# Scores 2 and 3 right behind the sums in four of six blocks, and a batch's fourth block with the last gate ahead of a convolution

## Chip, cores and metric

The kernel runs on one core of a Trainium2 chip. The metric is the device time of one execution in microseconds; the median of the runs counts. One execution was also recorded by the hardware profiler, and all rows below are of that one.

## What is computed

Capped softmax attention over 8 batches, 12 heads, 448 positions and 64 elements a head, and behind it a gated feed-forward layer with a causal convolution of five steps. `cap` is 30, so the largest score can be replaced by the cap in the exponential's shift.

```python
# attention
scores = cap * tanh(q @ k.T / sqrt(64) / cap)
attn = exp(scores - max(scores))
x = attn / (sum(attn) + 1e-9) @ v                # heads side by side: (8, 448, 768)
# layer
gate_pre[s] = sum over k of conv_w[k] * x[s - 4 + k]      # five steps, per column
gate = 1 / (1 + exp(-gate_pre))
out = (gate * (x @ w_val)) @ w_out
```

## The kernel before

The 48 pairs of heads are 48 blocks, six to a batch. For each block the kernel does these steps, each a function of its own in `fast_path`:

- `load`, `turn`: q and k come from memory (SyncE issues the DMAs) and are transposed on VectorE. `half_hi` (ScalarE) rounds them to the type that TensorE takes in one pass, `half_lo` (VectorE) makes the difference.
- `scores(p, i)`, i from 0 to 3: TensorE, keys on 112 rows, both heads at once on 64 rows of the array each; from block 13 on six matmuls each (high by high, high by low, low by high). They go to one of two PSUM tiles `pss`, so that scores 2 and 3 need what tanh 0 and 1 have read.
- `tanh`, `exp`: ScalarE, from `pss` to `pt`, then in place. There are six `pt` buffers.
- `add(p, 0)` adds the exponentials of i = 0 and 1, `add(p, 1)` those of 2 and 3, `add(p, 2)` these two: VectorE, in the tiles `pa0` and `pa1`.
- `attnv(p, i)`: TensorE, attention by v into `psa`; `sums`: a matmul with ones on the last `add` into `psz`, one for each head.
- `turn_sums`, `norm_recip`, `spread`, `norm_mul`: VectorE, the reciprocal of the sums, spread over the rows, times `psa`; the product `u` is x transposed. `x_hi` (ScalarE) and `x_lo` (VectorE) split x in two parts, `conv` (VectorE) makes the five steps of the convolution from `u`.

For a batch there is the layer: `sigmoid` of six gates (ScalarE), `val` (TensorE, six groups of 36 matmuls in two parts of 18), `gate` (VectorE, the product of the two), `gated_hi` (ScalarE) and `gated_lo` (VectorE), the two parts of the product, `out_part` (TensorE, six groups in even batches, eight in odd ones, each in two parts of 18), `store` (ScalarE copies from PSUM) and `store_out` (SyncE). `val` and `out_part` share two PSUM tiles `psf`. GpSimd has `keep_tail` alone, a copy once in two batches.

The order on each engine is written out by hand: every step gets a time in units of blocks from a table (`STEADY`, `SPLIT` and others; 0.62 in block p's table means p + 0.62), all are sorted by it, and each engine runs its own steps in that order and waits where data or a buffer is missing. So a block's steps lie between p - 1.9 (its load) and p + 1.9 (the end of its convolution), and the steps of three neighbours stand between one another. In block p's own stretch, from `scores(p, 0)` at p to the next block's, stand `attnv` and `sums` of block p - 1 (at p + 0.10 to p + 0.28), and with p + 0.36 and p + 0.74 two groups of 18 matmuls each of `val` or `out_part`; scores 2 and 3 stand between these two, at p + 0.62. `val` of a batch lies in the stretches of the next batch's first four blocks, `out_part` in those of its fourth to sixth and of the first after these. Behind block 47 there are no scores, and `val` and `out_part` of the last batch run by themselves.

For blocks from 12 on that are the first of their batch, `LATE_X` puts x's difference and the convolution late in the next block's stretch, where the sigmoids and two gates stand.

Of the kernel before, what the change touches and what calls it, by code (L numbers as in the profile page):

```python
# [82 lines left out]

SIXTH = PAIRED | {k: EARLY[k] for k in ("tq", "tk", "scores", "tanh", "exp")} | {"add": (0.38, 0.62)}

LATE_X = {"x_lo": 1.76, "conv": (1.78, 1.80, 1.83, 1.86, 1.89)}
NEARLY, NPAIRED, NPLAIN = 6, 11, 13

# [99 lines left out]
def fast_path(tc, io, u2, q, k, v, w_val, conv_w, w_out, out, capt):  # L188
# [8 lines left out]
    NPAIR = H // 2  # L197
    NP = B * NPAIR
# [12 lines left out]
    with ExitStack() as ctx:  # L211
# [82 lines left out]
        def half_hi(name, p):  # L294
            st = state[p]
            st[name, "h"] = scratch["qk"].tile([P, S], F32R, name=name + "h")
            nc.scalar.copy(st[name, "h"], st[name])

        def half_lo(name, p):
            st = state[p]  # L300
            st[name, "l"] = scratch["qk"].tile([P, S], F32R, name=name + "l")
            less(nc.vector, st[name, "l"], st.pop(name), st[name, "h"])
# [175 lines left out]
        tables = [EARLY if p < NEARLY else SIXTH if p == NEARLY else PAIRED if p < NPAIRED else STEADY if p < NPLAIN else SPLIT for p in range(NP)]  # L478
        for p in range(NPAIRED, NP):
            if p % NPAIR == 0:  # L480
                tables[p] = tables[p] | LATE_X

        def at(when, f, *a):
            events.append((when, len(events), f, a))

# [5 lines left out]
            q_hi=lambda p: half_hi("q", p), k_hi=lambda p: half_hi("k", p),  # L491
            q_lo=lambda p: half_lo("q", p), k_lo=lambda p: half_lo("k", p),
            scores=scores, tanh=tanh, exp=exp, add=add, av=attnv, sums=sums, turn_sums=turn_sums, recip=norm_recip,
            spread=spread, mul=norm_mul, x_hi=x_hi, x_lo=x_lo, conv=conv,
        )
        for p, table in enumerate(tables):
            for name, f in steps.items():
                x = table.get(name, ())
                if isinstance(x, tuple):
                    for i, y in enumerate(x):  # L500
                        at(p + y, f, p, i)
                else:
                    at(p + x, f, p)
        for b in range(B):
            t0 = NPAIR * b
            for d in range(NCC):
                sig = SIG_AT if b else SIG_FIRST
                y = (VAL if b else VAL_FIRST)[d]
                at(t0 + sig, sigmoid, b, d)
                for i in range(PARTS):  # L510
                    at(t0 + y + i * PART, val, b, d, i)
                done = t0 + max(y + PARTS * PART, sig + 0.17)
                at(done + 0.01, gate, b, d)

                last = d == NCC - 1
                at(done + (0.02 if last else 0.08), gated_hi, b, d)
                at(done + (0.03 if last else 0.12), gated_lo, b, d)
            if b % 2 == 0:
                at(t0 + KEEP_AT, keep_tail)
            for m, y in enumerate(OUT_ODD if b % 2 else OUT_LATE if b == B - 2 else OUT_EVEN):  # L520
                for i in range(PARTS):
                    at(t0 + y + i * PART / 2, out_part, b, m, i)
                at(t0 + y + 0.20, store, b, m)
                at(t0 + y + 0.40, store_out, b, m)
# [139 lines left out]
def kernel(tc, q, k, v, cap, w_val, conv_w, w_out, out):  # L664
    nc = tc.nc
    with tc.tile_pool(name="cap_pool", bufs=1) as pool, tc.tile_pool(name="io", bufs=2) as io:
        capt = pool.tile([P, 1], F32, name="capt")
        nc.sync.dma_start(capt, cap.rearrange("(o c) -> o c", o=1).partition_broadcast(P))

        pad = conv_w.shape[0] - 1  # L670
        u2 = [pool.tile([P, pad + q.shape[2]], F32, name=f"u{i}") for i in range(2)]
        for t, src in zip(u2, (q, k)):
            load_blocks(nc, t[:, pad:], src, 0)
        mag = pool.tile([1, 1], F32, name="mag")
        nc.vector.scalar_tensor_tensor(mag, capt[0:1], -1.0, capt[0:1], ALU.mult, ALU.max)
        small = pool.tile([1, 1], I32, name="small")
        nc.vector.tensor_scalar(small, mag, CAP_FAST, None, ALU.is_le)
        flag = nc.values_load(small, min_val=0, max_val=1)
        with tc.If(flag != 0) as cmp:
            fast_path(tc, io, u2, q, k, v, w_val, conv_w, w_out, out, capt)  # L680
        with cmp.Else():
            general_path(tc, q, k, v, w_val, conv_w, w_out, out, capt)
# [30 lines left out]
```

## Time and profile before

| | |
|---|---|
| median of 3 runs | 750.18 us (749.81 to 752.12) |
| the profiled execution | 749.64 us, span 747.9 us |
| TensorE busy, matmuls | 724.3 us |
| VectorE busy | 593.0 us |
| ScalarE busy | 537.7 us |
| mean granted clock of TensorE | 0.997 |

The span runs from the first to the last instruction of the profile; what lies around it belongs to the execution's time as well. Up to about 175 us the weights are prepared beside the first twelve blocks; from there to 688 us every stretch of a block is between 13 and 17 us long; behind 688 us comes the last batch's layer. An engine's busy time is the time covered by its instructions. A matmul counts from its start to its modelled end, and the next one starts before that end, so the distance between starts tells the rate. "Idle before" is time between an instruction and the one ahead of it, with the instruction that ended it.

### The profile page before, as it was taken

How to read it: one execution, taken by the hardware profiler on the slowest of the kernel's cores; microseconds unless marked ns; L12 is line 12 of the kernel's file. 1: busy time of each engine (PE TensorE's matmuls, PEld its weight loads, DVE VectorE, ACT ScalarE, POOL GpSimd, SP SyncE). 2: the span in 40 equal slices, each digit the busy share in tenths (PEclk: the TensorE clock that was granted, in tenths of full speed). 3: DMA queues.
4: the chain of work that ended last, by engine and by line, in shares of the span. 5: the costliest groups of instructions: out<-in, count | busy, mean ns of one | idle time of the engine just before them, and what ended most of it. 6: DMA issues, size and time to landing. Idle time of an engine off the chain costs nothing.

```text
span 747.9 us, 10860 instructions
## 1 busy us (share of the span) xinstructions
PE 724.3 (97%) x3972; PEld 488.3 (65%) x3972; DVE 593.0 (79%) x972; ACT 537.7 (72%) x708; POOL 9.0 (1%) x16
## 2 busy tenths in 40 slices
PE   5899998999999999999999999999999999999997
PEld 2333655566667776676777766667667775775997
DVE  2799899888987789987998679988898778997320
ACT  5899967778776697677857677687976659674311
POOL 0000001000000000000000000000000000000000
PEclk9999999999999999999999999999999999999999
DMA  6998867853223232233322333233322332210001
GB/s 105 234 212 195 209 166 149 232 110 73 37 51 79 70 73 37 61 82 71 67 46 61 88 69 54 38 81 73 59 49 62 80 79 41 49 35 22 22 21 67
DMA packets 241820, 63.75 MB, mean 85 GB/s; under 512 B 228448, under 2 KB 235616, under 8 KB 241760
## 3 DMA queue, kind: packets, MB, share of 16 engines
q1 hardware_dynamic: 241760, 62.98, 38.1%
q8 instruction: 33, 0.54, 0.3%
q14 instruction: 27, 0.22, 0.1%
HBM read 51.94 MB, written 11.01 MB: 84 GB/s over the span
## 4 chain that ended last, share of the span: by engine, by line
PE 43%; DVE 25%; ACT 16%; issue 4%; SPq 1%; DMA 1%; DVEq 0%; ACTq 0%
PE psf L461 8%; PE pss L312 7%; PE psf L463 7%; PE psf L462 7%; PE psa L349 6%; DVE pa L334 5%; ACT pt L320 5%; ACT pt L324 4%; DVE gate L411 4%; PE psz L361 3%; ACT gate L417 2%; PE psf L432 2%; DVE g_l L226 2%; PE psf L433 2%; PE psf L434 2%
## 5 line engine op out<-in xcount | busy, mean ns | idle before, releaser
L320 ACT ACTIVATE pt<-pss,rc 112x896 f32<-112x896 f32 x192 | 185.6, 1003 | 28.7 <-PE pss L312 28.7
L324 ACT ACTIVATE pt<-pt,capt 112x896 f32<-112x896 f32 x192 | 189.2, 1038 | 0.1
L349 PE MATMUL psa<-pt,vn 112*64 112x448 f32 x720 | 146.9, 546 | 0.0
L411 DVE SCALAR_TENSOR_TENSOR gate<-u,cw,gate 128x448 f32<-128x448 f32 x192 | 132.4, 690 | 5.8
L461 PE MATMUL psf<-wo,g_h 128*128 128x384 f32 x336 | 117.6, 350 | 0.0
L463 PE MATMUL psf<-wo,g_l 128*128 128x384 f32 x336 | 113.3, 337 | 0.0
L462 PE MATMUL psf<-wo,g_h 128*128 128x384 f32 x336 | 113.2, 337 | 0.0
L432 PE MATMUL psf<-xh,wv 128*128 128x448 f32 x288 | 108.8, 378 | 0.1
L434 PE MATMUL psf<-xl,wv 128*128 128x448 f32 x288 | 104.4, 362 | 0.0
L433 PE MATMUL psf<-xh,wv 128*128 128x448 f32 x288 | 104.3, 362 | 0.0
L334 DVE TENSOR_TENSOR pa<-pt 112x896 f32<-112x896 f32 x84 | 91.1, 1084 | 13.3 <-ACT pt L324 13.3
L349 PEld LDWEIGHTS psa<-pt,vn 112*64 112x64 f32 x720 | 47.4, 136 | 81.2 <-issue 69.8
L395 ACT CAST xh<-u 128x448 fp32r<-128x448 f32 x48 | 27.1, 565 | 77.1 <-DVE u L390 77.0
L461 PEld LDWEIGHTS psf<-wo,g_h 128*128 128x128 f32 x336 | 63.4, 189 | 22.0 <-issue 17.7
L369 DVE STREAM_TRANSPOSE zt<-psz 128x448 f32<-128x448 f32 x45 | 28.9, 641 | 56.3 <-PE psz L361 56.3
L432 PEld LDWEIGHTS psf<-xh,wv 128*128 128x128 f32 x288 | 54.0, 187 | 25.9 <-issue 18.3
L463 PEld LDWEIGHTS psf<-wo,g_l 128*128 128x128 f32 x336 | 63.6, 189 | 0.3
L462 PEld LDWEIGHTS psf<-wo,g_h 128*128 128x128 f32 x336 | 63.6, 189 | 0.0
L312 PE MATMUL pss<-qt,kt 64*112 64x448 f32 x208 | 49.6, 593 | 13.4 <-DVE guard L235 7.9
L441 ACT CAST g_h<-gate 128x448 fp32r<-128x448 f32 x48 | 26.3, 562 | 47.4 <-DVE gate L438 47.3
L469 ACT COPY osb<-psf 128x384 f32<-128x384 f32 x56 | 26.7, 478 | 45.9 <-PE psf L463 43.2
L312 PE MATMUL pss<-qh,kh 64*112 64x448 f32 x280 | 58.5, 412 | 0.0
(74 smaller groups left out, 904.2 us busy)
## 6 DMA issues: line engine op xcount, KB each, us to landing
vn<-in_v_dram SPq DMA_DIRECT2D x96, 112.0 KB, 2.6
out_dram<-osb SPq DMA_DIRECT2D x56, 192.0 KB, 1.9
qn<-in_q_dram SPq DMA_DIRECT2D x188, 56.0 KB, 2.5
kn<-in_k_dram SPq DMA_DIRECT2D x188, 56.0 KB, 2.4
w_raw<-in_moe_w_val_dram SPq DMA_DIRECT2D x12, 384.0 KB, 4.5
w_late<-in_moe_w_val_dram SPq DMA_DIRECT2D x12, 384.0 KB, 4.3
w_raw<-in_moe_w_out_dram SPq DMA_DIRECT2D x12, 384.0 KB, 3.7
w_late<-in_moe_w_out_dram SPq DMA_DIRECT2D x12, 384.0 KB, 4.7
```

The lines of the kernel that those rows point to most:

```text
L312: nc.tensor.matmul(ps[:CH, j, :S], st[x][r, c], st[y][r], start=(n == 0), stop=(n == len(parts) - 1))
L320: nc.scalar.activation(st["p", i], st.pop(("s", i)), AF.Tanh, scale=rc8[:CH])
L324: nc.scalar.activation(t, t, AF.Exp, scale=capt[:CH])
L334: nc.vector.tensor_tensor(st["a", i], st["p", 2 * i], st["p", 2 * i + 1], op=ALU.add)
L349: nc.tensor.matmul(st["o"][r, :S], vloads[p][:, j, i], t[:, j], start=(i == 0), stop=(i == NKT - 1))
L411: nc.vector.scalar_tensor_tensor(g, u[:, i:i + S], cw[:, hp, i:i + 1], g, ALU.mult, ALU.add)
L432: nc.tensor.matmul(o, w_h, xh, start=(c == 0), stop=False)
L433: nc.tensor.matmul(o, w_l, xh, start=False, stop=False)
L434: nc.tensor.matmul(o, w_h, xl, start=False, stop=(c == NCC - 1))
L461: nc.tensor.matmul(o, g_h[:, d, s], w_h, start=(d == 0), stop=False)
L462: nc.tensor.matmul(o, g_h[:, d, s], w_l, start=False, stop=False)
L463: nc.tensor.matmul(o, g_l[:, d, s], w_h, start=False, stop=(d == NCC - 1))
```

## The change

Tables are added and, from block 13 on, laid over the old ones. `together(p)` is true for blocks 14 to 47 that are the first, third, fifth or sixth of their batch. For these, scores 2 and 3 move from 0.62 to 0.31, behind the sums of the block before; tanh and exp 2 and 3 and the two last additions follow them in the same stretch. For the block ahead of such a one, x's difference moves ahead of the next block's q and k differences, and its convolution is parted: step 0 in its old stretch, steps 1 to 4 one stretch later, behind the transposes of q and k and ahead of `turn_sums`. For the third block of a batch (`GATE_FIRST`) x's difference and the whole convolution move a little, to 1.66 to 1.71, which in the fourth block's stretch is behind the batch's last gate and its `gated_lo` at 0.63 and 0.65; before, they stood between 0.58 and 0.70, around these two. No step is added or left out.

```diff
+TOGETHER = {
+    "scores": (0.0, 0.05, 0.31, 0.32),
+    "tanh": (0.06, 0.13, 0.34, 0.36),
+    "exp": (0.22, 0.29, 0.47, 0.53),
+    "add": (0.52, 0.60, 0.61),
+}
+NEXT_TOGETHER = {
+    "turn_sums": 1.41, "recip": 1.42, "spread": 1.43, "mul": 1.44, "x_hi": 1.45, "x_lo": 1.54,
+    "conv": (1.58, 2.16, 2.17, 2.18, 2.19),
+}
+PREPARE_TOGETHER = {"q_hi": -0.69, "k_hi": -0.68, "q_lo": -0.44, "k_lo": -0.43}
+
+GATE_FIRST = {"x_lo": 1.66, "conv": (1.67, 1.68, 1.69, 1.70, 1.71)}
 LATE_X = {"x_lo": 1.76, "conv": (1.78, 1.80, 1.83, 1.86, 1.89)}
...
+        def together(p):
+            return NPLAIN < p < NP and p % NPAIR not in (1, 3)
+
+        for p in range(NPLAIN, NP):
+            if together(p - 1):
+                tables[p] = tables[p] | PREPARE_TOGETHER
+            if together(p):
+                tables[p] = tables[p] | TOGETHER
+            if p % NPAIR == 2:
+                tables[p] = tables[p] | GATE_FIRST
+            if together(p + 1):
+                tables[p] = tables[p] | NEXT_TOGETHER
```

## Rows read from the trace of the kernel before

**Rows 1.** The page's part 1: busy time, share of the span, instructions.

```profile
PE 724.3 (97%) x3972; PEld 488.3 (65%) x3972; DVE 593.0 (79%) x972; ACT 537.7 (72%) x708; POOL 9.0 (1%) x16
```

**Rows 2.** Waits, 180 to 748 us: total, times, longest.

```profile
PE psz L361 <- DVE pa L331: 3.4, 7, 1.7
```

**Rows 3.** TensorE's timeline, turns 22 and 23: start, length, instruction, [idle before].

```profile
324.02 3.23 PE L349 MATMUL psa<-pt,vn 112*64 112x448 f32 x16
327.08 0.92 PE L361 MATMUL psz<-pa,ones 112*64 112x448 f32 x4
327.93 0.45 PE L461 MATMUL psf<-wo,g_h 128*128 128x384 f32 x1
...
331.26 0.46 PE L312 MATMUL pss<-qh,kh 64*112 64x448 f32 x2
...
332.68 0.44 PE L461 MATMUL psf<-wo,g_h 128*128 128x384 f32 x1
```

**Rows 4.** TensorE's timeline, turn 28: start of 36 output matmuls, next scores.

```profile
403.65 0.44 PE L461 MATMUL psf<-wo,g_h 128*128 128x384 f32 x1
...
410.12 0.46 PE L312 MATMUL pss<-qh,kh 64*112 64x448 f32 x2
```

**Rows 5.** TensorE's timeline, turn 47: sums, scores, output matmuls.

```profile
676.95 0.92 PE L361 MATMUL psz<-pa,ones 112*64 112x448 f32 x4
677.80 0.46 PE L312 MATMUL pss<-qh,kh 64*112 64x448 f32 x2
...
679.22 0.44 PE L461 MATMUL psf<-wo,g_h 128*128 128x384 f32 x1
```

**Rows 6.** TensorE's timeline, turn 25: value matmuls behind sums, next scores.

```profile
355.22 0.47 PE L432 MATMUL psf<-xh,wv 128*128 128x448 f32 x1
...
359.03 0.46 PE L312 MATMUL pss<-qh,kh 64*112 64x448 f32 x2
```

**Rows 7.** TensorE's timeline, the last batch: start of its value and output matmuls.

```profile
696.35 0.36 PE L432 MATMUL psf<-xh,wv 128*128 128x448 f32 x1
...
717.95 0.34 PE L461 MATMUL psf<-wo,g_h 128*128 128x384 f32 x1
```

**Rows 8.** ScalarE's timeline, turn 22: tanh 0 and 1.

```profile
311.56 1.92 ACT L320 ACTIVATE pt<-pss,rc 112x896 f32<-112x896 f32 x2
```

**Rows 9.** TensorE's timeline, turn 22: `attnv` and sums of block 21.

```profile
310.29 3.23 PE L349 MATMUL psa<-pt,vn 112*64 112x448 f32 x16
313.61 0.97 PE L361 MATMUL psz<-pa,ones 112*64 112x448 f32 x4
```

**Rows 10.** The page's part 6: DMA issues, count, size, median us to landing.

```profile
qn<-in_q_dram SPq DMA_DIRECT2D x188, 56.0 KB, 2.5
```

**Rows 11.** VectorE's timeline, turns 20 to 22: `turn_sums` of 19, additions of 20, 21.

```profile
286.39 0.61 DVE L369 STREAM_TRANSPOSE zt<-psz 128x448 f32<-128x448 f32 x1
...
296.51 1.09 DVE L334 TENSOR_TENSOR pa<-pt 112x896 f32<-112x896 f32 x1 [0.31 <-ACT pt L324]
...
311.34 1.09 DVE L334 TENSOR_TENSOR pa<-pt 112x896 f32<-112x896 f32 x1 [1.35 <-ACT pt L324]
312.46 1.09 DVE L331 TENSOR_TENSOR pa<-pa,pa 112x896 f32<-112x896 f32 x1
```

**Rows 12.** VectorE's timeline, the last batch: a `gated_lo` straight behind its `gate`.

```profile
708.61 0.63 DVE L226 TENSOR_TENSOR g_l<-gate,g_h 128x448 fp32r<-128x448 f32 x1 [0.63 <-ACT g_h L441]
```

**Rows 13.** TensorE's timeline, turn 48: `attnv` and sums of block 47.

```profile
682.56 3.23 PE L349 MATMUL psa<-pt,vn 112*64 112x448 f32 x16
687.51 0.97 PE L361 MATMUL psz<-pa,ones 112*64 112x448 f32 x4 [1.72 <-DVE pa L331]
```

**Rows 14.** VectorE's timeline, turns 47 and 48: convolution of 46, last addition of 47.

```profile
682.39 2.85 DVE L411 SCALAR_TENSOR_TENSOR gate<-u,cw,gate 128x448 f32<-128x448 f32 x4
...
686.27 1.09 DVE L331 TENSOR_TENSOR pa<-pa,pa 112x896 f32<-112x896 f32 x1
```

**Rows 15.** Windows: busy time (count) of five engines, granted clock, DMA share, GB/s.

```profile
690.00:691.00 1.00, 1.00 (x5) 1.00 (x4) 0.97 (x2) 0.00 (x0) 0.00 (x0) 0.50 0.00 0
```

## The prediction

> Names: block p is one pair of heads (48 of them, six to a batch), V stands for the matmuls of the value product (`val`), O for those of the output product (`out_part`). "Turn p" is the stretch from `scores(p, 0)` to `scores(p+1, 0)`; in it TensorE also runs `attnv` and `sums` of block p-1. A "together" block is one of the first, third, fifth or sixth of its batch, from block 14 on.
>
> **What bounds the kernel now.** I read the page's part 1 first: TensorE is busy 97% of the span [rows 1]. That alone says little, since a matmul that is pipelined behind another counts as busy, so the next view was the waits from 180 us on: seven waits of a TensorE matmul for the sums' operand, 3.4 us together, 1.7 of them in one place [rows 2], and hardly another idle nanosecond. So TensorE is the bound through the attention part and what can be gained is (a) time in which it counts as busy but does not stream, and (b) those waits. For (a) the timeline of TensorE is read by the distance from one group's first start to the next group's: `attnv` 3.06, `sums` 0.85, O (18 matmuls) 3.33, scores (12) 1.42 [rows 3].
>
> **Part 1: one change of kind less in a together turn.** TensorE streams matmuls of three kinds: scores on 64 rows, `attnv` and `sums` into 64 columns, V and O on the whole array. Before, a turn runs scores, sums, V or O, scores, V or O: each border is a change. After, it runs scores, sums, scores, V or O twice. What a change costs can be read off, for the trace has both forms. Two O groups with scores between take 3.33 each [rows 3]; where two stand back to back, 36 matmuls take 410.12 - 403.65 = 6.47 [rows 4]. So a group of O that does not open behind another kind spares 2 x 3.33 - 6.47 = 0.19 to 0.20. The border sums to scores, new in every together turn, stands in turn 47 already: 0.85 from the sums to the scores and 1.42 for the scores [rows 5], the same as sums to O and as scores behind O [rows 3]. So that border costs what the one it replaces costs, and one change in five goes, at 0.20. V: 18 matmuls behind the sums take 3.81 [rows 6], while 108 behind an O take 21.60, 3.60 for 18 [rows 7]; 0.21 by the same reasoning, for V on V and for V on O. There are 23 together turns. Turn 47 gains nothing, since nothing stood between its sums and scores; the six of third blocks (14, 20, 26, 32, 38, 44) come into part 2; the other 16 spare 16 x 0.20 = 3.2 us, if nothing waits. Bounds: 3.0 to 3.4 by the reading of the rows.
>
> What could wait in these turns. `scores(p, 2)` and `(p, 3)` take the two score banks back from tanh 0 and 1, and move some 3.3 us forward, so ScalarE must be done with these by the end of the sums; queued behind a waiting matmul stands all of TensorE. The tightest case I find is the fifth block's turn: both tanh start at 311.56 and take 1.92, so end at 313.48, against sums that start at 313.61 and take 0.9 [rows 8, 9]: 1.0 us to spare. On ScalarE tanh 2 and 3 now run before x's rounding (`x_hi`), with the exponentials behind it; the work of a turn is the same, and it ends earlier. On VectorE x's difference now comes before the next block's q and k differences, so these stand behind a wait for `x_hi`; by adding up the durations `x_hi` is there 0.2 to 0.3 us before VectorE asks: nothing, or 0.2 a turn on an engine which in O turns has over 1 us to spare. Four of five convolution steps of a block move one turn on, ahead of `turn_sums`, where VectorE stood idle for the sums. Output copies move behind the exponentials, about 1.5 us later, and with them SP's output DMAs and the loads queued behind these; a load of q lands in 2.5 us [rows 10] and is issued about a block ahead, so I cost that at nothing; without that cover it would be the 1.5 us a turn. In odd batches three O groups of the fifth and sixth block share two banks, and the third needs the first one's copy: 0.3 to 0.5 us to spare, worth a few tenths a batch if I am wrong. GpSimd's one step, `keep_tail`, and all loads keep their places in the written order.
>
> **Part 2: third and fourth blocks, where VectorE sets the pace.** From turn 20 to turn 22 VectorE is almost without a pause: `turn_sums` of block 19 starts at 286.39, the last addition of block 21 ends at 312.46 + 1.09 = 313.55, and the idle time named between is 0.31 and 1.35, both for an exponential of ScalarE [rows 11]. The sums of 21 start on its result, at 313.61, 3.32 behind the `attnv` where 3.06 is normal [rows 3, 9]. Between these two points VectorE has the same instructions after the change: the four convolution steps (2.85 us) that leave the third turn fall into the fourth, and the two additions (about 2.1) of the third block go the other way. So the end moves only by idle time. The exponentials come early enough now: in the third turn since scores 2 and 3 come early, in the fourth since the last gate stands ahead of x's difference and the convolution, so that ScalarE, whose tanh queue behind the gate's rounding, is let go about 1.7 us sooner. That removes 1.66. Against it, `gated_lo` now twice stands directly behind its `gate`, with nothing in between to cover ScalarE's rounding; such a pair costs 0.63 of idle time [rows 12], 1.26 for two, and a third one with a transpose between perhaps 0.1. Left: 1.66 - 1.36 = 0.3, say 0.25 a batch, as TensorE's own sums are then only some 0.2 behind. Six such places: 1.5 us. Bounds: TensorE could take at most the change of kind and its wait, 0.20 + 0.26 with some 0.15 of waits on score banks, so 6 x 0.6 = 3.6; on the other side, one more uncovered pair of 0.63 in each makes it 6 x 0.38 = 2.3 lost. The sums' wait of the third turn itself (block 19's additions behind a gate) stands as before, since nothing ahead of it in the second turn changes: the moved convolutions end about 1.9 us before VectorE is asked for the sums.
>
> **Part 3: the end of the attention part.** In turn 48 the last sums start at 687.51, where 682.56 + 3.06 = 685.62 is due: 1.9 us [rows 13]. They wait for the last addition, 686.27 to 687.36, which stands behind four convolution steps of block 46 (682.39 to 685.24) [rows 14]. After, these steps stand behind the additions, and x's rounding behind the last tanh. The last scores end about 679.4 [rows 5]; from there one tanh, the rounding (some 0.5) and two exponentials (taken as long as tanh, 0.96 each) [rows 8] bring ScalarE to about 683.0, two additions (1.1 each) VectorE to about 685.3, 0.3 before the sums are due. So the 1.9 us go. And there is more: behind this wait the granted clock is 0.50, the lower of the two levels (1.2 GHz), in the window that I asked for [rows 15]; from the sums to the first V it is 696.35 - 687.51 = 8.84 [rows 7, 13] where 0.85 + 6.47 = 7.32 would do [rows 3, 4]: 1.5 us. The clock fell behind the longest idle time of this part and behind none of the six short ones. Without the wait I expect it not to fall, so the term is 1.9 + 1.5 = 3.4. Late next is the last block's x: by the added durations its difference is ready about 1 us before the first V wants it. Bounds: 0 to 3.4.
>
> The Trainium skill, "TensorE: Matmul & The Clock Gate", section "Seeing it yourself", warns that clock events in traces of this chip were seen to be unreliable. By that the lower clock might be a slip of the record, and the sum 1.5 us less gain, 743.0. The distances just given stretch with it, so here the trace goes against the warning.
>
> **The sum.** The profiled execution took 749.64 us (span 747.9), 0.54 under the median of 750.18. 749.64 - 3.2 - 1.5 - 3.4 = 741.5; with the median's 0.54 it would be 742.0. I say 741.8.
>
> **Rivals.**
> A, the end is not freed: an exponential or the `attnv` is late in its place, 1.9 and 1.5 stay: 749.64 - 3.2 - 1.5 = 744.9. For it: only 0.3 us to spare. Against: before, the exponential was ahead of the addition by as much as the convolution took.
> B, the fourth block's queue on VectorE pays for the moved convolution, and the kernel gets slower. The four steps (2.85) stand there ahead of `turn_sums`, `u`, `gate` and the additions that the fifth turn's sums want. If VectorE had to pause at the end of the third turn (the two gates wait for V there, which now runs in one piece), they would not be absorbed but come on top: in full 6 x 2.85 = 17.1, giving 758.6. It decides from 1.35 us a batch (8.1 / 6), and is measurably slower from 1.7. Against it: at the second of these gates V is due about 1.2 us before VectorE arrives.
> C, scores 2 and 3 wait for tanh 1 behind the sums. With a margin of 1.0 in fifth blocks, a ScalarE that is 1.5 us later there costs 0.5 x 6 = 3.0: 744.5; all 22 turns together would lose the whole gain at 0.37 us each.
> D, the change of kind is paid elsewhere (the border sums to scores has a single example, without a V or O group behind its sums in the same turn): 749.64 - 1.5 - 3.4 = 744.7.
>
> **How the numbers follow.** Forecast 0.67, A 0.10, B 0.12 (of it 0.06 slower, 0.05 no change, 0.01 faster), C 0.06 (0.02 no change, 0.01 slower), D 0.05. Differences under 0.3%, 2.25 us, can't be told from none. Faster: 0.67 + 0.10 + 0.01 + 0.03 + 0.05 = 0.86; no change 0.07; slower 0.07. The range runs from parts 1 and 2 near their better bounds (749.64 - 3.4 - 3.0 - 3.4 = 739.8) to A, C or D with part 2 a little below nothing, 745.8.
>
> **What would show it.** TensorE's timeline: in together turns 1.42 for scores behind sums and 6.47 for two O, 7.4 for two V. Sums of third blocks' turns still waiting about 0.2 to 0.3, those of fifth blocks' turns about 0.3; no scores waiting for banks. In turn 48, sums straight behind `attnv` and the granted clock at 1.00 until the last stores. Wrong would be: TensorE's idle time for tanh (C), a wait at the fifth turn's sums over 1 us (B), a low clock anywhere in the attention part.

## The result, and the profile after

| | before | after |
|---|---|---|
| median, runs beside each other | 750.14 us (749.81 to 752.12, 4 runs) | 743.84 us (741.32 to 745.13, 4 runs) |
| ratio | | 0.9907, 95% interval 0.9891 to 0.9923 |
| the profiled execution | 749.64 us, span 747.9 | 741.32 us, span 739.6 |
| TensorE busy | 724.3 us | 717.1 us |

The kernel is 0.9% faster; 741.8 was forecast, in a range from 739.8 to 745.8. On five more rounds beside the kernel before it was 742.71 against 749.99 (0.9904, 0.9881 to 0.9926). The three terms did not all come as forecast, though: the second gave 0.7 us less than forecast, in the profiled execution 0.9 us from ahead of the change made up for that, and of the third 1.5 us turned out to belong to one execution and not to the kernel.

First, TensorE's timeline of the changed kernel in turn 23 (start, length, instruction): `attnv`, sums, then scores straight behind them, two O groups in one piece, the next scores. This answers to [rows 3] and [rows 4].

```profile
322.10 3.23 PE L363 MATMUL psa<-pt,vn 112*64 112x448 f32 x16
325.16 0.92 PE L375 MATMUL psz<-pa,ones 112*64 112x448 f32 x4
326.01 0.46 PE L326 MATMUL pss<-qh,kh 64*112 64x448 f32 x2
...
327.41 0.44 PE L475 MATMUL psf<-wo,g_h 128*128 128x384 f32 x1
...
333.86 0.46 PE L326 MATMUL pss<-qh,kh 64*112 64x448 f32 x2
```

From sums to scores 0.85, scores 1.40, both O groups 333.86 - 327.41 = 6.45: one change of kind less, at the price forecast. The turn takes 13.16 us from its `attnv` to the next, where 13.41 stood before. No matmul of the scores is named as waiting behind 180 us.

Second, the waits from 180 us to the end, as in [rows 2], show what came instead: no wait of 1.7 any more, but more and longer ones of the other sums.

```profile
PE psz L375 <- DVE pa L345: 3.5, 9, 0.6
```

Three of these nine are new: they stand in turns 22, 34 and 46, the fifth turns in which an even batch's layer runs (called even batches below). In turn 22 the distance from `attnv` (308.07) to its sums is 3.85, against 3.32 in [rows 9]:

```profile
311.92 0.97 PE L375 MATMUL psz<-pa,ones 112*64 112x448 f32 x4 [0.62 <-DVE pa L345]
```

The profile names 0.62 of this as idle. From here on, the wait of sums is how far their distance from `attnv` exceeds the usual 3.06: 0.79 here and 0.26 before.

Third, turn 48, with the sums 3.05 behind `attnv` and V right behind two O groups (to be held against [rows 7] and [rows 13]), and the granted clock of those stretches (windows: busy time of PE, weight loads, VectorE, ScalarE, GpSimd, then the clock, DMA share, GB/s), which answers to [rows 15]:

```profile
677.49 3.23 PE L363 MATMUL psa<-pt,vn 112*64 112x448 f32 x16
680.54 0.92 PE L375 MATMUL psz<-pa,ones 112*64 112x448 f32 x4
...
687.77 0.36 PE L446 MATMUL psf<-xh,wv 128*128 128x448 f32 x1
```

```profile
681.00:685.00 4.00, 4.00 (x25) 3.61 (x21) 3.79 (x8) 0.00 (x0) 0.00 (x0) 1.00 0.02 4
685.00:689.00 4.00, 4.00 (x24) 3.92 (x24) 3.26 (x6) 1.92 (x4) 0.00 (x0) 1.00 0.13 49
```

From `attnv` to the first V it is 10.28, where 696.35 - 682.56 = 13.79 stood before [rows 7, 13].

A measure for all that follows is the distance between two starts on TensorE, `attnv` of block 13 and `attnv` of block 47. It holds every changed turn up to block 47's `attnv` and nothing ahead of the change, and repeats within 0.1 us in all profiled executions of one kernel: before 491.74, 491.75 and 491.67 in three, after 487.52 and 487.42 in two. So of the 8.3 us between the two profiled executions, 4.2 were gained there, 3.5 behind it up to the first V, 0.9 came from ahead of block 13's `attnv`, where nothing was changed (190.82 against 189.96), and -0.3 are left for the rest.

| | forecast, 6 batches or all turns | measured in the first two profiles |
|---|---|---|
| changes of kind, first and sixth blocks (10) | 2.0 | 2.2 |
| change of kind and wait in fifth blocks' turns (6) | 1.2, wait in part 2 | odd batches 0.72, even batches -0.92 |
| third and fourth blocks' turns, with the fifth's wait | 1.5 | third 1.32, fourth 0.92 |
| end, wait | 1.9 | 1.9 |
| end, clock | 1.5 | 1.6, but see below |

(The second and third row belong together: 2.7 forecast, 2.0 measured.) The third turns' 0.22 each is the change of kind. The fourth turns' 0.15 each is the short wait for a score bank that the prediction had in its bound: the fifth block's first twelve scores took 310.29 - 308.73 = 1.56 before, the second six from 309.50 on, right behind the end of a tanh at 309.45, and take 308.07 - 306.66 = 1.41 now.

### The profile page after: what moved, and what is told of

The parts are those of the page before. It is cut to its first block, busy times and chain, and to the rows that moved or that the text cites. A ratio compares the mean times of both kernels' runs of the same rounds, so it can differ in the third digit from the quotient of the medians.

```text
span 739.6 us, 10858 instructions
## 1 busy us (share of the span) xinstructions
PE 717.1 (97%) x3972; PEld 488.8 (66%) x3972; DVE 593.0 (80%) x972; ACT 534.7 (72%) x708; POOL 9.0 (1%) x16
## 4 chain that ended last, share of the span: by engine, by line
PE 52%; DVE 21%; ACT 13%; issue 2%; SPq 1%; DMA 0%; DVEq 0%; ACTq 0%
PE pss L326 9%; PE psf L475 8%; PE psf L477 7%; PE psf L476 7%; DVE gate L425 7%; PE psa L363 6%; PE psf L446 4%; PE psf L447 4%; PE psf L448 4%; ACT pt L334 3%; PE psz L375 3%; DVE pa L348 3%; ACT gate L431 3%; ACT pt L338 2%; DVE pa L345 2%
## 5 line engine op out<-in xcount | busy, mean ns | idle before, releaser
L425 DVE SCALAR_TENSOR_TENSOR gate<-u,cw,gate 128x448 f32<-128x448 f32 x192 | 130.6, 680 | 5.7
L475 PE MATMUL psf<-wo,g_h 128*128 128x384 f32 x336 | 115.7, 344 | 0.0
L476 PE MATMUL psf<-wo,g_h 128*128 128x384 f32 x336 | 112.4, 335 | 0.0
```

The source lines that it names most:

```text
L425: nc.vector.scalar_tensor_tensor(g, u[:, i:i + S], cw[:, hp, i:i + 1], g, ALU.mult, ALU.add)
L475: nc.tensor.matmul(o, g_h[:, d, s], w_h, start=(d == 0), stop=False)
L476: nc.tensor.matmul(o, g_h[:, d, s], w_l, start=False, stop=False)
```

## The experiments

### The end, and TensorE's clock

Only the last block changed:

```diff
-            return NPLAIN < p < NP and p % NPAIR not in (1, 3)
+            return p == NP - 1
...
-            if p % NPAIR == 2:
-                tables[p] = tables[p] | GATE_FIRST
```

> Only the last block is changed (scores 2 and 3, tanh, exponentials, additions of block 47, and the convolution of block 46 parted). M: the wait at the last sums (1.9) goes and the lower clock behind it (1.5) with it: 749.6 - 3.4 = 746.2, granted clock 1.00 up to the last stores. Rival E, the clock falls there for a reason of its own: 1.9 alone, 747.7, and 0.50 near 690 us still. Rival A, the wait stays: 749.6.

747.18 against 749.99 (0.9968, 0.9950 to 0.9987), 2.8 us less. In its trace the last sums stand 3.06 behind their `attnv`, and the distance between the two `attnv` is that of the kernel before, 491.78. The median lies between the two forecasts of 746.2 and 747.7, and can't tell them apart. The other half of the change can:

```diff
-            return NPLAIN < p < NP and p % NPAIR not in (1, 3)
+            return NPLAIN < p < NP - 1 and p % NPAIR not in (1, 3)
```

> All of the change but the last block's. M: 741.5 + 3.4 = 744.9, the last sums wait 1.7 us or more again and the granted clock falls to 0.50 behind them. Rival E: 743.4, the wait without the lower clock.

744.52 us (0.9932, 0.9911 to 0.9952), and the last sums wait as they did before, but the clock stays up behind them. TensorE's timeline and a window over the O groups behind the wait:

```profile
679.74 3.23 PE L363 MATMUL psa<-pt,vn 112*64 112x448 f32 x16
684.68 0.97 PE L375 MATMUL psz<-pa,ones 112*64 112x448 f32 x4 [1.71 <-DVE pa L345]
691.96 0.36 PE L446 MATMUL psf<-xh,wv 128*128 128x448 f32 x1
```

```profile
685.60:691.90 6.30, 6.30 (x38) 6.30 (x37) 5.33 (x10) 1.05 (x2) 0.00 (x0) 1.00 0.08 31
```

12.22 from `attnv` to V, not 13.8, so rival E holds and M does not. The median of 744.52 would not have told: it lies close to M's 744.9, but M and E start from 741.5, and the whole change had a median of 742.71 beside it, to which 1.9 adds up to 744.6. The kernel before was then run and profiled twice more:

> The kernel before once more, for TensorE's clock behind the last sums' wait of 1.9 us. M: it falls to 0.50 there as in the first profile, and from the last attnv to the first V it is 13.8. Rival E: the clock falls behind such a wait only in some executions, since with the same wait of 1.88 in the run without the last block's part it stayed at 1.00; then the distance is 12.3 in this one.

> The kernel before a third time, for TensorE's clock behind the last sums' wait of 1.9 us, which is the same in every execution. So far it fell once (first profile) and did not twice (before_again, no_end). E: no sure consequence of the wait; the distance from the last attnv to the first V is 12.2 when it stays at 1.00 and 13.8 when it falls.

Both times the wait was there (1.72 and 1.71 named) and the clock stayed at 1.00 (the windows of these two executions, the O groups behind the wait):

```profile
687.00:693.00 6.00, 6.00 (x36) 5.92 (x35) 4.93 (x10) 1.05 (x2) 0.00 (x0) 1.00 0.09 33
```

```profile
692.90:699.30 6.40, 6.40 (x39) 6.38 (x38) 5.39 (x10) 1.05 (x2) 0.00 (x0) 1.00 0.09 33
```

Distances 12.21 and 12.22. One execution in four with this wait had the lower clock behind it. The wait is worth 1.9 us in every execution, the clock's 1.5 belongs to the one that happened to be profiled.

### Where the time varies

The changed kernel, unaltered:

> The changed kernel once more, for where its time varies from run to run (741.3 to 745.1 so far, mean clock 0.998 to 0.994). Theory M (three terms: changes of kind, third and fourth turns, end): a calm execution takes 741 to 742. Spread, theory S1: TensorE's clock falls once more in some executions, behind the sums' waits of 0.8 us in the fifth turns of even batches; then a slower one shows windows of 0.50 behind one of these, 1.5 us each. Theory S2: it is lost ahead of 175 us, where weights are prepared and nothing was changed; then the last sums start at the same distance from the sums of block 12 as in the first profile, 502 us.

742.71 us, from 741.48 to 744.47. The profiled one of these runs took 744.03, against 741.32 for the first profile of the same kernel. The two agree to 0.1 us between the two `attnv`; block 13's `attnv` starts at 192.70 and 189.96, 2.74 apart, and that is the whole difference. Ahead of it the windows show (first row this execution, second row the first one):

```profile
129.80:136.60 6.80, 5.63 (x16) 1.77 (x18) 6.10 (x10) 6.80 (x9) 0.00 (x0) 0.50 0.66 175
```

```profile
129.00:136.00 7.00, 5.39 (x30) 1.91 (x28) 6.76 (x10) 7.00 (x9) 0.00 (x0) 1.00 0.63 169
```

S2 holds, and 2.5 of the 2.74 are lost there: TensorE's clock falls to its lower level in the stage in which the weights are prepared, in some executions and not in others. Around the place where it falls, scores wait twice for ScalarE's tanh. These two waits stand in all fourteen profiled executions, with a fall or without, so they alone don't decide it, and what does stays open. In the first execution of the kernel before, where the clock did not fall there (TensorE's timeline):

```profile
129.03 1.01 PE L312 MATMUL pss<-qt,kt 64*112 64x448 f32 x4 [1.42 <-ACT pt L320]
131.65 1.01 PE L312 MATMUL pss<-qt,kt 64*112 64x448 f32 x4 [1.61 <-ACT pt L320]
```

The third execution of the kernel before has 0.50 there as well and starts block 13's `attnv` at 195.40, where 190.82 and 189.49 stand in the two without. It took 752.81, and the second one 747.23. Not all of that is the clock's: of the 5.9 us between the two starts, 2.9 were lost from 125 us on, and 2.1 between 93 and 104 us, at a granted clock of 1.00. Eight of the fourteen profiled executions of all these kernels have a lower clock between 129 and 140 us, and none between 180 and 680 us, so S1 falls. Two executions with 1.00 from 20 us to the last stores compare best: 747.23 before and 741.32 after, 5.9 less. That is 4.2 and 1.9, with -0.2 left over, and it is what the change itself is worth by these traces.

### The fourth block's gate

```diff
-            if p % NPAIR == 2:
-                tables[p] = tables[p] | GATE_FIRST
```

> The change without GATE_FIRST: in the fourth turn the last gate stands between the convolution's steps again. M: the exponentials come some 1.7 us later, of which 1.3 fit ahead of the addition, and the idle 0.63 behind the gate goes: within 0.3 us a batch, 740 to 744 in all. Rival G, the earlier gate is what carries the third and fourth turns: 1.3 to 1.7 us a batch more, 749 to 751, with VectorE idle for an exponential ahead of the additions.

747.67 us (0.9975, 0.9958 to 0.9993), 492.33 between the two `attnv`: 4.8 worse than the change, and 0.6 worse than before the change; the end's 1.9 us are kept. M's "within 0.3 a batch" is wrong; G has the direction, but 0.8 a batch came, not 1.3 to 1.7, and not at its place: against the change 0.95 is lost in each fourth turn and 0.2 in odd batches' fifth turns, where the cause stays open, and 0.5 is won back in even ones. The additions are no later than before: the sums of the fifth turns wait 0.25, in even batches less than the 0.79 with the gate ahead. What waits is the first O group, in the fourth turn (TensorE's timeline, turn 21):

```profile
306.06 0.44 PE L475 MATMUL psf<-wo,g_h 128*128 128x384 f32 x1
...
309.17 0.44 PE L475 MATMUL psf<-wo,g_h 128*128 128x384 f32 x1 [0.23 <-ACT g_h L455]
...
309.83 0.45 PE L477 MATMUL psf<-wo,g_l 128*128 128x384 f32 x1
310.20 0.46 PE L326 MATMUL pss<-qh,kh 64*112 64x448 f32 x2
```

The group takes 310.20 - 306.06 = 4.14 instead of 3.34, and the scores behind it lose the 0.15 again. Its last three matmuls need both parts of the last gate's product. The parted convolution has pushed VectorE back by some 0.8 us in this turn (it takes up the sums at 301.76, 0.9 behind the end of TensorE's group, where it was 0.1 before), and without `GATE_FIRST` the gate stands behind x's difference and two convolution steps besides. The prediction had named the additions as the ones who want this gate, and not O. So the parted convolution needs `GATE_FIRST`; whether the convolution in its old place needs it too, no run here shows.

### GpSimd's copy in even batches

> The change, with GpSimd's copy of the last rows (keep_tail, even batches from the second on) held back by one GpSimd step that reads the x of block 21, 33 or 45 and so waits for VectorE's product in the fifth turn. Theory K: in even batches' fifth turns the sums wait 0.79 instead of 0.26 because the copy now runs beside x's difference and the convolution's first step on VectorE, which take 0.92 and 0.70 there against 0.62 and 0.45; then the wait falls to 0.25 to 0.30, turns 22, 34 and 46 from 14.03 to 13.5, and from block 13's attnv to block 47's it is 487.5 - 3 x 0.53 = 485.9. Rival K2, the two groups of 18 matmuls or ScalarE's copy in these turns are the cause: wait and turn stay as they are.

```diff
-                at(t0 + KEEP_AT, keep_tail)
+                at(t0 + 10.56 if b else t0 + KEEP_AT, keep_tail, b)
...
+                nc.gpsimd.tensor_scalar(mark, gates[b * NPAIR + 9][1][:, PAD:PAD + 1], 1.0, 0.0, ALU.mult, ALU.add)
```

485.78, with turns 22, 34 and 46 at 13.47 to 13.49 and their sums' wait at 0.23: K's numbers, and K2 falls. 741.21 us (0.9883, 0.9859 to 0.9906). GpSimd's and VectorE's timelines of the changed kernel in turn 21 show what was removed. GpSimd's copy of the high parts is let go by ScalarE's last rounding, and x's difference and the first convolution step beside it are longer:

```profile
304.88 0.89 POOL L462 TENSOR_SCALAR g_h<-g_h 128x384 fp32r<-128x384 f32 x1 [184.19 <-ACT g_h L455]
305.73 0.88 POOL L462 TENSOR_SCALAR g_l<-g_l 128x384 fp32r<-128x384 f32 x1
```

```profile
305.31 0.92 DVE L240 TENSOR_TENSOR xl<-u,xh 128x448 fp32r<-128x448 f32 x1
306.15 0.70 DVE L423 TENSOR_SCALAR gate<-u,cw 128x448 f32<-128x448 f32 x1
```

With the copy elsewhere the same two are 0.62 and 0.45:

```profile
306.63 0.62 DVE L240 TENSOR_TENSOR xl<-u,xh 128x448 fp32r<-128x448 f32 x1
307.16 0.45 DVE L424 TENSOR_SCALAR gate<-u,cw 128x448 f32<-128x448 f32 x1
```

0.30 and 0.25 a time. Before, the copy ran beside convolution steps (two took 1.77 there, 1.40 in an odd batch), and VectorE waited for an exponential right behind them, 1.35 in the even batch and 1.72 in the odd one (kernel before, VectorE's timeline, turn 28), so that it cost nothing:

```profile
395.71 1.09 DVE L334 TENSOR_TENSOR pa<-pt 112x896 f32<-112x896 f32 x1 [1.72 <-ACT pt L324]
```

The Trainium skill, "GPSIMD Engine Reference", section "1. Specifications", says that GpSimd's way to SBUF is shared with VectorE, with contention where a VectorE instruction has two SBUF inputs or runs in a two-port mode. The first is true of the difference, and its 0.92 agrees; whether the convolution's first step, with one tensor and one column of weights as its inputs, runs in such a mode no run here shows.

### VectorE's idle time between the third and the fifth turn

> As keep_late, and VectorE's two uncovered waits for ScalarE's rounding (0.63 each) get work in between: the third turn's gate moves ahead of the last addition, the fourth turn's last gated_lo behind x's difference. Theory M (VectorE sets the pace from the third to the fifth turn, its idle time is what counts): the fifth turns' sums no longer wait, 13.24 instead of 13.5 in even batches, 16.38 in odd ones instead of 16.62, some 484.4 from block 13's attnv to block 47's; 738 to 739 in a calm execution. Rival: the additions wait for the exponentials instead, then the distance stays at 485.9.

```diff
-                at(done + 0.01, gate, b, d)
+                at(t0 + 8.605 if b and d == 3 else done + 0.01, gate, b, d)
...
-                at(done + (0.03 if last else 0.12), gated_lo, b, d)
+                at(t0 + 9.664 if b and last else done + (0.03 if last else 0.12), gated_lo, b, d)
```

484.28, no fifth turn's sums wait, 13.16 to 13.20 and 16.32 us. What stands forecast for TensorE is met to 0.12 us, though not all of VectorE's waiting is covered: of 1.43 in three waits, one of 1.02 is left, in the third turn. The median of 741.39 (0.9876, 0.9849 to 0.9903) is not below that of keep_late: its runs lie between 737.91 and 742.58, the lowest at a mean clock of 1.0, the highest at 0.992. This fits the spread of the weights' stage, but only one of these runs was profiled (740.63), and it had no fall there.

> The change, but the convolution's steps 1 to 4 stay in their old turn, behind the additions, instead of moving one turn on. M: VectorE's work between the third and the fifth turn's sums is the same, so 487.5 from block 13's attnv to block 47's within 1 us, with VectorE idle longer for the sums in O turns. Rival B2, moving these steps is needed: gates come 2.8 us later in the third turn, ScalarE's tanh of the fourth stand behind the rounding of these, and 0.5 to 1.5 us a batch are lost, 490 to 496.

```diff
-    "conv": (1.58, 2.16, 2.17, 2.18, 2.19),
+    "conv": (1.58, 1.64, 1.65, 1.67, 1.70),
```

484.34, so 3.2 better than the change, and both expectations are wrong. 739.31 us (0.9861, 0.9830 to 0.9892). Leaving the four steps where they were takes nothing from the other parts and removes the fifth turns' wait, even with GpSimd's copy in its old place. VectorE's timeline of the third turn, first of the changed kernel, then of this one, tells why:

```profile
292.04 0.62 DVE L452 TENSOR_TENSOR gate<-psf,gate 128x448 f32<-128x448 f32 x1
293.29 0.63 DVE L240 TENSOR_TENSOR g_l<-gate,g_h 128x448 fp32r<-128x448 f32 x1 [0.63 <-ACT g_h L455]
293.83 0.62 DVE L452 TENSOR_TENSOR gate<-psf,gate 128x448 f32<-128x448 f32 x1
294.37 0.63 DVE L305 STREAM_TRANSPOSE qt<-qn 128x448 f32<-128x448 f32 x1
295.17 0.62 DVE L240 TENSOR_TENSOR g_l<-gate,g_h 128x448 fp32r<-128x448 f32 x1 [0.17 <-ACT g_h L455]
```

```profile
292.41 0.62 DVE L452 TENSOR_TENSOR gate<-psf,gate 128x448 f32<-128x448 f32 x1
292.95 2.84 DVE L425 SCALAR_TENSOR_TENSOR gate<-u,cw,gate 128x448 f32<-128x448 f32 x4
295.70 0.62 DVE L240 TENSOR_TENSOR g_l<-gate,g_h 128x448 fp32r<-128x448 f32 x1
```

The four steps stand between a gate and its `gated_lo`, and cover ScalarE's rounding: 0.80 of idle time less, against waits of 0.25 and 0.79 in the fifth turns. From the end of the third turn's last addition to the end of the fifth turn's VectorE takes 28.09 us in even batches and 27.51 in odd ones, where the changed kernel takes 28.87 and 28.32: 0.8 less in both. So M was right that VectorE's amount of work between these points is the same; what it left out is its other half, that idle time counts. The second of the two gates comes 2.0 us later in its turn, and none of the losses that B2 gave for that came: no matmul of the third or fourth turn waits longer.

The last pair of runs uses what was learnt. In the third turn the gate with index 2 goes behind block 1's additions:

```diff
-                at(done + 0.01, gate, b, d)
+                at(t0 + 8.07 if b and d == 2 else done + 0.01, gate, b, d)
...
-                at(done + (0.02 if last else 0.08), gated_hi, b, d)
+                at(t0 + 8.30 if b and d == 2 else done + (0.02 if last else 0.08), gated_hi, b, d)
...
-                at(done + (0.03 if last else 0.12), gated_lo, b, d)
+                at(t0 + 8.45 if b and d == 2 else t0 + 9.664 if b and last else done + (0.03 if last else 0.12), gated_lo, b, d)
```

> As conv_stays, and in the third turn the gate with index 2, which stands ahead of block 1's last two additions, moves behind them (its rounding behind exp 1, its gated_lo behind the product for x). Theory M (VectorE sets the pace between the third and the fifth turn's sums, and its idle time there is what the fifth turn's sums wait for): the third turn's sums come 0.41 to 0.48 sooner and no longer wait. In odd batches VectorE has that much to spare, so they gain 0.48 each. In even batches it has nothing to spare (wait 0.00 with conv_stays, GpSimd's copy beside it), so the fifth turn's sums wait 0.4 instead: 484.3 - 3 x 0.48 = 482.9 from block 13's attnv to block 47's. Rival P, TensorE sets the pace throughout: 484.3 - 3 x 0.48 - 3 x 0.41 = 481.7 with no wait in any fifth turn.

481.25, no wait in any third or fifth turn, 736.62 us (0.9826, 0.9805 to 0.9848). That is P's number, but the last line of the edit also put the fourth turn's last `gated_lo` behind x's difference, which takes away VectorE's last named wait of 0.63 for a rounding; so this run tells nothing of M and P. Without that part (the edit against gate2_late):

```diff
-                at(t0 + 8.45 if b and d == 2 else t0 + 9.664 if b and last else done + (0.03 if last else 0.12), gated_lo, b, d)
+                at(t0 + 8.45 if b and d == 2 else done + (0.03 if last else 0.12), gated_lo, b, d)
```

> gate2_late also had the fourth turn's last gated_lo behind x's difference, which its expectation did not name and which gives VectorE some 0.46 us to spare in even batches; so it could not tell M from P. Here gated_lo stays where conv_stays has it, and only gate 2 of the third turn, with its rounding and gated_lo, moves behind block 1's additions. M: in even batches the third turn gains 0.41 and the fifth turn's sums wait 0.35 to 0.45 instead of 0.00; odd batches gain 0.48: 482.7 to 482.9 from block 13's attnv to block 47's. P: no wait in any fifth turn, 481.7.

482.83 (740.66 us, a single execution), with waits of 0.44, 0.46 and 0.44 in turns 22, 34 and 46 and none in turns 16, 28 and 40. That is M: what the third turn's sums gain in even batches is lost two turns on. The gate that now stands behind the third turn's additions is done before the fifth turn's all the same, and the idle time of 0.63 is still there.

And `gate2_late` with the copy held back as in keep_late:

> gate2_late with GpSimd's copy held back as in keep_late. M and P: 481.7, no wait of 0.2 or more in third or fifth turns; in a calm execution some 2.7 us less than conv_stays, 736 to 737. If holding the copy back is worth nothing here, 482.9 as without it (M is wrong on the copy then).

481.40, which is gate2_late's distance: with the covered `gated_lo` there already is room enough, and holding the copy back adds nothing to it in this order. 736.16 us (0.9831, 0.9805 to 0.9856), from 734.26; the profiled execution has a span of 732.5. Both versions beat both kernels. Against the one before it is 13 us; the one after was not run beside them, and the distances make it 6 us (487.5 against 481.3). Between the two versions nothing can be told.

## Why the prediction was right, and where it was not

**Part 1** was right in mechanism and size: 0.19 to 0.25 for each turn. Scores behind the sums cost what they cost in turn 47, and rival D falls. Rival C falls too: no scores wait for a bank.

**Part 2** was right in its mechanism (VectorE sets the pace between the third and the fifth turn), by which keep_late, covered_keep and gate2_only were forecast within 0.15 us each, and wrong in size: with the change of kind of the fifth turn 2.7 were forecast and 2.0 came. The step that failed is "VectorE has the same instructions after the change" with "So the end moves only by idle time". The same instructions do not take the same time: in even batches two of them now run beside GpSimd's copy, which costs 487.52 - 485.78 = 1.7 us by keep_late. The prediction had looked at `keep_tail` and found only that it keeps its place in the written order. Its place in time is set by ScalarE's last rounding, which the change moved from just ahead of a wait, where its cost was hidden, to a place with no wait behind it. In odd batches, where there is no copy, the turns gained 0.22, 0.15 and 0.25, and the sums' wait of 0.25 stayed.

So the 0.7 is what two errors of opposite sign leave. VectorE's stretch from the third turn's last addition to the fifth's, which takes 28.7 us before in every batch, was to shrink by 0.25; it shrank by 0.39 in odd batches and grew by 0.16 in even ones. The 1.66 of idle time that the forecast took away six times was read in an even batch; in an odd one it is 0.30 and 1.72. And the tanh behind the last gate came 0.8 us sooner after `attnv`, not 1.7; the wait for the exponential went even so, because VectorE itself, with the moved steps ahead, comes to the additions 1.7 later.

"Against it, `gated_lo` now twice stands directly behind its `gate`" was right: 0.63 twice and 0.17 in the trace, against 1.36 in the sum. That it is the moved convolution which uncovers those of the third turn (0.63 and 0.17, both gone from the named waits in conv_stays) was not seen, and so the move itself was costed at nothing ("where VectorE stood idle for the sums"). It costs 487.52 - 484.34 = 3.2 us, by conv_stays.

**Part 3**: the wait went as worked out, sums 3.05 behind `attnv`, 1.9 us, and rival A falls. "Without the wait I expect it not to fall, so the term is 1.9 + 1.5" is the step that failed here: of four profiled executions with the wait, the clock fell in the one that the term was read from. The warning of the Trainium skill, "TensorE: Matmul & The Clock Gate", section "Seeing it yourself", was about the record. Here the record was true, as it is 13.79 from `attnv` to V with the fall and 12.22 without; the mistake was to take one execution's clock for the kernel's.

**The sum** of 741.5 against the profiled 741.32 is partly luck: part 2 gave 0.7 less, 0.9 came from ahead of block 13, and the clock's 1.5 was gained only because the profiled execution of the kernel before had the fall. Against medians the gain is 6.3 to 7.3, not 8.1.

**Rival B** did not come: the sums of the fifth turn waited under 0.9 us, and under the 1 us that was to show it. But no_gate_first shows how near it was: with `GATE_FIRST` left out the moved steps cost more than the whole change of kind brings, through the O group, not through the additions.

## What to carry to other kernels

When two engines hand a value to and fro (gate, rounding, difference), look for work that stands between and is moved away: the pair's waiting time appears on the engine that sets the pace. A step without an edit can still change its neighbours, if a faster chain lets it go at another time; ask for each engine with one or two steps what they run beside, before and after. And a distance between two instructions on the bounding engine, ahead of and behind all that was changed, tells a gain of 0.3 us where the total varies by more than three.

## What the runs showed of the hardware

TensorE's granted clock fell to 0.50 in this program in places and not always: behind a wait of 1.7 us in one of four executions, and between 129 and 140 us in eight of fourteen, in the kernel before as in the changed ones. The second of these accounts for a part of the spread from run to run: block 13's `attnv` starts between 189.49 and 191.79 us in the six profiled executions without a fall between 129 and 140 us, and between 191.38 and 195.40 in the eight with one.

V behind O is no change of kind: in turn 24 of the changed kernel O and V together take 6.93, where 3.33 and 3.81 stand for the two behind other kinds, and 0.2 is saved as with two groups of O.

A VectorE instruction beside GpSimd's copy took longer: 0.92 instead of 0.62 for a difference of two tensors, 0.70 instead of 0.45 for a product of one tensor and a column.
